# Attention and a routed mixture of experts: a slot table for one expert only, with one scattered row a token tile

## The chip, the cores and the metric

The kernel runs on one core of a Trainium2 chip. The metric is the time of one execution on the device in microseconds (us). Five engines run their own instruction streams: PE (matrix products, with its weight loads shown as PEld), DVE (vector), ACT (scalar functions), POOL (here mostly the issuer of indirect DMAs) and SP (the issuer of plain DMAs). They meet through semaphores.

## The reference

Attention over 8 batches, 8 heads, 576 tokens, head size 64, with a causal window of 32 (first four heads) or a dilated window (reach 128, every fourth key, last four heads). Its output, 4608 tokens of 512 numbers, goes through a mixture of 8 experts, each token through its best two:

```python
logits = x @ w_gate
noise_scale = np.log1p(np.exp(x @ w_noise))
noisy_logits = logits + noise_scale * noise
top2 = np.argpartition(-noisy_logits, 2, axis=1)[:, :2]
top2_l = np.take_along_axis(noisy_logits, top2, axis=1)
top2_l = top2_l - top2_l.max(-1, keepdims=True)
top2_w = np.exp(top2_l)
top2_w /= top2_w.sum(-1, keepdims=True) + 1e-09
for e in range(E):
    for k in range(2):
        mask = top2[:, k] == e
        h = np.maximum(x[mask] @ w1[e], 0.0)
        out[mask] += top2_w[mask, k, None] * (h @ w2[e])
```

## The kernel before

**Attention** runs in 24 steps, four units of 1152 tokens with six steps each (three of each mask type). A step has scores (PE L348), their maximum (DVE L353), exponentials, transposes (PE L368, evicted by ACT L371 as `pt`), the product with the values (PE L388, `o`), the division (DVE L395 to L400), transposes of the result (PE L414, ACT L416) and the gate's logits (PE L436). A step has two places, called slots here and numbered `kb`, between which other work is put: `at(kb, f)` runs `f` in slot `kb`, and generators on the list `gens` are advanced a few instructions at a time by `micro`.

**Gates.** `gate(t0, n)` takes `n` tiles of 128 tokens: it finds the two best experts of each token, counts tokens per expert by a product with a triangular matrix (so every token gets a rank within its expert), and then writes, for each tile and each of the two choices, one row of eight integers per token into the table `tab` in DRAM at row (expert, rank): the four places of the token's attention output in the scratch `xs`, the weight, the token's number. That is an indirect DMA issued by POOL (L577) with a one-element memset ahead of it (L576): two a tile, 72 in all. The gates start at slots 17, 29, 39, 41, 51 with 9, 9, 6, 3, 6 tiles; one of 3 tiles is left for the end of attention. Rows of the table that no token takes are filled beforehand (`setup_c`, L267 to L288; the tokens' places are computed in one block of DVE work, `setup_b`, L226 to L261).

**Experts.** Expert 0 is a fixed one; the other seven are taken in the order of their token counts, and each has a fixed capacity of 1216 down to 1152 slots (an overflow path, which the data here doesn't enter, handles the rest). An expert has three blocks of 3, 4 and 3 tiles. `up` (L764) makes 12 products for each of 8 slices `f` of the hidden size (three for each fourth of the model size, since operands are split in a high and a low part), ACT takes the relu into `hh` (L768) and DVE the low part `hl` (L769). `down_tile` (L805) makes 24 products for a tile, DVE multiplies by the weight into `y` (L814), and POOL adds the rows to the output by an indirect DMA with addition (`out_rows`, L782, with a memset L781). PSUM holds three buffers for `up` and two for `dn`.

**Fetching tokens.** For expert 0 SP reads rows of the table into `ixf`, POOL gathers (four indirect DMAs a tile, L710), and PE transposes (L730). For another expert SP reads its part of the table (`idx_dma`: L688, L691, L693), DVE copies it into place (L698), POOL gathers (L716, one indirect DMA for 32 tokens), and DVE transposes in 32 by 32 squares (L733). ACT and DVE split the result into `x` (L735, L736). Expert 0's first block is fetched during the last unit of attention.

**What sets the order.** Each engine's instructions stand in the order of the code. After attention a clock of column counts (`tick`, 2400 columns a us) decides where planned work (`plan(t, f)`) is put between the products of `up` and `down`.

Of the kernel before, what the change touches and what calls it, by code (L numbers as in the profile page):

```python
# [12 lines left out]
I32 = mybir.dt.int32  # L13
# [27 lines left out]
US_W2 = 3.0, 3.5  # L41
US_X = (17, 52)
# [3 lines left out]
def attention_moe_kernel(ctx, tc, qt, kp, kd, vpl, vdl, w_gate, w_noise, noise, w1, w2, out, CAPS=(1216, 1216, 1216, 1184, 1184, 1152, 1152, 1152), SPLITS=(0, 384, 896)):  # L46
# [19 lines left out]
    xq = xs.rearrange("r (q d) -> (r q) d", d=128)  # L66
    tab = dram.tile([E * ET, TC], I32, name="tab")

# [4 lines left out]
    ixp = ctx.enter_context(tc.tile_pool(name="ixp", bufs=3))  # L73
# [121 lines left out]
    i8 = gat.tile([128, NG, E], F32, name="i8")  # L195
# [5 lines left out]
    def setup_a():  # L201
# [7 lines left out]
        gpsimd.iota(i8, pattern=[[0, NG], [1, E]], base=0, channel_multiplier=0,  # L209
                    allow_small_or_imprecise_dtypes=True)  # L210
        gpsimd.iota(ebase, pattern=[[ET, E]], base=0, channel_multiplier=0,
                    allow_small_or_imprecise_dtypes=True)
        gpsimd.tensor_copy(base, ebase)
        for e in range(E):
# [4 lines left out]
    def setup_b():  # L219
# [3 lines left out]
        t = tokc[:, :, 5]  # L223
        v, s, i0, r, z, a = (acon.tile([128, 2, NT], I32, name=f"tc{i}") for i in range(6))
        gpsimd.iota(v[:, 0].rearrange("p (s j) -> p s j", j=3), pattern=[[0, 12], [128, 3]], base=0, channel_multiplier=1)
        vector.tensor_scalar(a[:, 0], t, 2, None, op0=OP.bitwise_and)  # L226
        vector.tensor_scalar(v[:, 1], t, 2, None, op0=OP.logical_shift_right)
        vector.scalar_tensor_tensor(v[:, 1], a[:, 0], 72.0, v[:, 1], op0=OP.mult, op1=OP.add)
        for u in range(U):
            c = slice(NG * u, NG * u + NG)  # L230
            gpsimd.iota(s[:, 0, c].rearrange("p (s j) -> p s j", j=3), pattern=[[768, 3], [0, 3]],
                        base=768 * (6 * u + 3), channel_multiplier=0)
            vector.tensor_scalar(a[:, 0, c], t[:, c], float(TU * u + S), 144.0, op0=OP.is_ge, op1=OP.mult)
            vector.scalar_tensor_tensor(v[:, 1, c], v[:, 1, c], -288.0 * u, a[:, 0, c], op0=OP.add, op1=OP.add)
            vector.memset(s[:, 1, c], 4608 * u)
# [227 lines left out]


    tabw = []
    LG = {}

    def gate_front(u, st):
        if st == 0:
# [677 lines left out]
```

## Time and profile before

| | |
|---|---|
| median of 3 runs | 1205.72 us (1190.08, 1205.72, 1205.93) |
| the profiled execution | 1184.15 us; its span in the trace 1182.5 us; mean granted clock 0.941 |
| attention, until expert 0's first product | 0 to 265.6 us |
| expert 0 | 265.6 to 418.8 us |
| expert 1 | 418.8 to 540.4 us |
| each later expert | some 106 to 111 us |

Rows of the stretches list, behind the two ends and the length in us, the busy us and the number of instructions of PE, PEld, DVE, ACT and POOL, then the granted clock of PE (1.00 is full), the busy share of the DMA engines and GB/s. Rows of groups list line, engine, operation, tiles, count, then busy us and mean ns, then the engine's idle time ahead of them and what ended most of it. Rows of waits list engine, tile and line, what was waited for, us in total, times, longest.

### The profile page before, as it was taken

To read this page: it belongs to the slowest core of one execution; us is meant where nothing else is said; L and a number is where in the kernel's file an instruction comes from. 1 tells how busy PE (TensorE), PEld (TensorE's weight loads), DVE (VectorE), ACT (ScalarE), POOL (GpSimd) and SP (SyncE) were. 2 spreads that over 40 slices of the span, in tenths; PEclk is the share of its full clock that TensorE was granted. 3 is DMA by queue.
4 is the path that set the end of the run, shared out by engine and by line. 5 is a ranking of instruction groups with operands and counts; after the bars stand their busy time and mean duration, and the time that the engine had idled before them with its cause. 6 is when DMAs were issued, how large, how long until landed. Compare 5 with 4: busy or idle time off the path is not lost. (4 is left out here: it accounts for less than half of the span.)

```text
span 1182.5 us, 18050 instructions
## 1 busy us (share of the span) xinstructions
PE 1026.8 (87%) x7278; PEld 865.2 (73%) x7279; DVE 467.6 (40%) x1077; ACT 298.9 (25%) x540; POOL 519.9 (44%) x637
## 2 busy tenths in 40 slices
PE   5885737667589899899999998999999999999996
PEld 3663535446378787788889887978888898878885
DVE  6762524344223335243432433343434334332321
ACT  6442413342111223122222312231222223122210
POOL 5006062526456453745644562465246445624012
PEclk9997879777699999899999998999999999999998
DMA  8794538437033233352434333343424353432223
GB/s 287 266 331 182 206 126 299 150 127 271 11 62 63 70 94 94 63 115 52 118 56 108 83 89 63 81 107 74 106 47 116 68 97 91 84 94 45 54 28 45
DMA packets 70967, 133.71 MB, mean 113 GB/s; under 512 B 29520, under 2 KB 29568, under 8 KB 69600
## 3 DMA queue, kind: packets, MB, share of 16 engines
q1 hardware_dynamic: 48176, 93.22, 23.4%
q0 software_dynamic: 22704, 39.30, 18.6%
q8 instruction: 58, 0.95, 0.3%
q14 instruction: 29, 0.24, 0.1%
HBM read 92.19 MB, written 40.29 MB: 112 GB/s over the span
## 5 line engine op out<-in xcount | busy, mean ns | idle before, releaser
L764 PE MATMUL up<-x,w1h 128*128 128x512 f32 (+4 forms) x1536 | 403.4, 349 | 43.1 <-issue 16.8
L764 PEld LDWEIGHTS up<-x,w1h 128*128 128x128 f32 x1536 | 278.9, 194 | 70.3 <-DVE hl L769 18.8
L716 POOL DMA_INDIRECT g<-xs,ixi x258 | 259.7, 1007 | 107.9 <-issue 84.2
L764 PE MATMUL up<-x,w1l 128*128 128x384 f32 (+4 forms) x768 | 266.3, 347 | 1.7 <-issue 1.6
L782 POOL DMA_INDIRECT out_rows<-y,ixs x67 | 106.3, 1586 | 310.6 <-DVE y L814 260.9
L805 PE MATMUL dn<-w2h,hh 128*128 128x512 f32 x576 | 227.4, 395 | 3.3 <-issue 1.8
L805 PE MATMUL dn<-w2l,hh 128*128 128x512 f32 x576 | 226.1, 393 | 4.4 <-issue 4.4
L805 PE MATMUL dn<-w2h,hl 128*128 128x512 f32 x576 | 225.9, 392 | 3.0 <-issue 3.0
L769 DVE SCALAR_TENSOR_TENSOR hl<-up,hh 128x384 fp32r<-128x384 f32 (+2 forms) x192 | 105.7, 556 | 299.0 <-ACT hh L768 205.9
L768 ACT ACTIVATE hh<-up 128x384 fp32r<-128x384 f32 (+4 forms) x192 | 92.7, 498 | 320.7 <-PE up L764 197.0
L764 PEld LDWEIGHTS up<-x,w1l 128*128 128x128 f32 x768 | 149.1, 194 | 12.2 <-issue 1.8
L805 PEld LDWEIGHTS dn<-w2h,hl 128*128 128x128 f32 x576 | 109.3, 190 | 27.4 <-issue 4.3
L805 PEld LDWEIGHTS dn<-w2h,hh 128*128 128x128 f32 x576 | 109.5, 190 | 26.9 <-issue 4.3
L805 PEld LDWEIGHTS dn<-w2l,hh 128*128 128x128 f32 x576 | 109.5, 190 | 26.6 <-issue 4.7
L577 POOL DMA_INDIRECT tab<-en,si x72 | 70.2, 975 | 115.1 <-DVE den L397 55.5
L814 DVE TENSOR_SCALAR y<-dn,ixs 128x512 f32<-128x512 f32 x63 | 46.9, 748 | 127.8 <-PE dn L805 121.5
L735 ACT CAST x<-xr 128x512 fp32r<-128x512 f32 x67 | 40.5, 605 | 175.8 <-DVE xr L733 144.1
L649 DVE TENSOR_TENSOR w1l<-ws,w1h 128x1024 fp32r<-128x1024 f32 x32 | 38.7, 1218 | 75.3 <-ACT w1h L647 67.7
L388 PE MATMUL o<-vp,pt 128*32 128x130 f32 x576 | 32.1, 296 | 30.3 <-ACT pt L371 16.7
L710 POOL DMA_INDIRECT g<-xs,ixf x40 | 38.3, 958 | 42.8 <-DMA kt<-in_kp 21.7
L647 ACT CAST w1h<-ws 128x1024 fp32r<-128x1024 f32 x32 | 33.1, 1048 | 92.8 <-DMA ws<-in_moe_w 92.8
L733 DVE STREAM_TRANSPOSE xr<-g 128x512 f32<-128x512 f32 x67 | 45.8, 683 | 20.5 <-DMA g<-xs,ixi 16.2
(184 smaller groups left out, 839.4 us busy)
## 6 DMA issues: line engine op xcount, KB each, us to landing
ws<-in_moe_w SPq DMA_DIRECT2D x64, 512.0 KB
out_rows<-zero SPq DMA_DIRECT2D x38, 256.0 KB
vd<-in_vdl SPq DMA_DIRECT2D x24, 390.0 KB
vp<-in_vpl SPq DMA_DIRECT2D x16, 585.0 KB
xs<-x SPq DMA_DIRECT2D x24, 384.0 KB
qt<-in_qt SPq DMA_DIRECT2D x14, 576.0 KB
kt<-in_kd SPq DMA_DIRECT2D x16, 320.0 KB
g<-xs,ixi POOLq DMA_INDIRECT x258
```

What stands on the lines that cost most here:

```text
L577: ins = gpsimd.indirect_dma_start(out=tab, out_offset=bass.IndirectOffsetOnAxis(ap=si[:, kq, t:t + 1], axis=0), in_=en[:, kq, t], in_offse ...
L649: return lambda: vector.tensor_tensor(b, s, a.bitcast(F32), op=OP.subtract)
L710: gpsimd.indirect_dma_start(out=g[0:rn, c], out_offset=None, in_=xq[0:rows], in_offset=bass.IndirectOffsetOnAxis(ap=IX[0][0][0:rn, t, c:c ...
L716: gpsimd.indirect_dma_start(out=g[:, j], out_offset=None, in_=xq, in_offset=bass.IndirectOffsetOnAxis(ap=IX[e][1][:, r0 // 32 + j:r0 // 32 ...
L733: vector.transpose(xr[:, :, 0:rn].rearrange("p c (g t) -> p g c t", t=32), g[:, 0:n].rearrange("p g (c d) -> p g c d", d=32))
L735: scalar.copy(xh[:, :, o:o + rn], xr[:, :, 0:rn])
L764: tensor.matmul(p[:, 0:n], lhsT=a[:, 128 * f:128 * f + 128], rhs=b[:, kc, 0:n], start=(i == 0), stop=(i == 11))
L768: scalar.activation(hh[:, f, 0:n], p[:, 0:n], AF.Relu)
L769: vector.scalar_tensor_tensor(hl[:, f, 0:m], p[:, 0:m], 0.0, hh[:, f, 0:m].bitcast(F32), op0=OP.max, op1=OP.subtract)
L782: ins = gpsimd.indirect_dma_start(out=out, out_offset=bass.IndirectOffsetOnAxis(ap=sc[0:rn, t, 1:2], axis=0), in_=y[0:rn], in_offset=None, ...
L805: tensor.matmul(p[0:rn], lhsT=a[:, f, o:o + rn], rhs=b[:, f % 2], start=(i == 0), stop=(i == 23))
L814: vector.tensor_scalar(y[0:rn], p[0:rn], wsc, None, op0=OP.mult)
```

## The change

- The table is for expert 0 only (`tab0`). A gate scatters one row a token: to its slot if one of its two choices is expert 0, else to a row beyond the table that nobody reads. That is one indirect DMA a tile (L624), 36 in all.
- There are four gates during attention in place of five (slots 17, 29, 43, 51 with 9, 9, 9, 6 tiles), and the one at the end.
- A gate also keeps each token's (expert, rank) and weight in SBUF and writes the weights of all experts to a DRAM array `wtab` by SP (L592).
- For the other seven experts the slots are found without a table. For each of the 72 pairs of a tile and a choice, two matrices are made: `A`, 128 by 128, one where a token's rank modulo 128 is the column's number, and `V`, 128 by 70, the token's number in the column of its expert and tile of slots, else zero. The product of `A` transposed and `V`, added up over all 72 in one PSUM bank `acc`, is the token of each slot. `A` is made by DVE (odd pairs, L730) or by two ACT instructions (even pairs, L732, L733), `V` by DVE (L734); the product is L739. `slots()` is run through by planned steps during expert 0, and ends with some 59 DVE instructions (L746 to L771) that turn tokens into places in `xs`.
- An expert's gathers (now L878) then take their indices from SBUF: the reads of the table by SP and the 28 copies L698 go. For the weights there is one more gather a tile (`wq` from `wtab`, L884), 67 in all, planned ahead of the `up` of their block.
- Expert 0's first block is gathered in halves of a tile, in twice as many slots; expert 1's gathers are planned from 64.1 instead of 51 on the planner's clock after expert 0's start, and closer together (5 for 7, 15 for 21).
- `token_places` replaces `setup_b`: a generator in small pieces, from slot 8. `setup_c` fills 1280 rows instead of all.

The core of the diff:

```diff
-        for t in range(n):
-            for kq in range(2):
-                gpsimd.memset(spacer, 0.0)
-                ins = gpsimd.indirect_dma_start(
-                    out=tab, out_offset=bass.IndirectOffsetOnAxis(ap=si[:, kq, t:t + 1], axis=0),
-                    in_=en[:, kq, t], in_offset=None)
...
+        for t in range(n):
+            gpsimd.memset(spacer, 0.0)
+            ins = gpsimd.indirect_dma_start(
+                out=tab0, out_offset=bass.IndirectOffsetOnAxis(ap=si[:, t:t + 1], axis=0),
+                in_=en[:, t], in_offset=None)
...
+    def slots():
...
+        acc = late["mps"].tile([128, NO], F32, name="acc", tag="acc", bufs=1)
+        for i in range(m + 3):
+            if i < m:
+                if i % 4 == 0:
+                    av = late["stage"].tile([128, 4, 256], F32R, name="av", tag="ws")
+                A, V = av[:, i % 4, 0:128], av[:, i % 4, 128:128 + NO]
+                if i % 2:
+                    vector.tensor_scalar(A, iof, lo[:, i:i + 1], None, op0=OP.is_equal)
+                else:
+                    scalar.activation(A, iof, AF.Abs, bias=nlo[:, i:i + 1])
+                    scalar.activation(A, A.bitcast(F32), AF.Relu, scale=-1.0, bias=one)
+                vector.tensor_scalar(V, iof[:, 0:NO], d[:, i:i + 1], tokf[:, i // 2:i // 2 + 1],
+                                     op0=OP.is_equal, op1=OP.mult)
+                ops[i] = (A, V)
+            if i >= 3:
+                A, V = ops.pop(i - 3)
+                tensor.matmul(acc, lhsT=A, rhs=V, start=(i == 3), stop=(i == m + 2), skip_group_check=True)
+            yield
...
+    def weights(e, t):
+        c, rn = NC * (e - 1) + t, TLS[e][t][1]
+        gpsimd.indirect_dma_start(out=late["wq"][0:rn, c:c + 1], out_offset=None, in_=wtab,
+                                  in_offset=bass.IndirectOffsetOnAxis(ap=late["wi"][0:rn, c:c + 1], axis=0))
...
-                later(2 + i if bi == 0 else 1, lambda t=t: gather(0, t))
+                for h in range(2):
+                    later(1 + 2 * i + h, lambda t=t, h=h: gather(0, t, (2 * h, 2 * h + 1)))
...
-    for t0, n, kb in ((0, 9, 17), (9, 9, 29), (18, 6, 39), (24, 3, 41), (27, 6, 51)):
+    for t0, n, kb in ((0, 9, 17), (9, 9, 29), (18, 9, 43), (27, 6, 51)):
...
+            bulk = others()
+            for i in range(135):
+                plan(start + BULK[0] + BULK[1] * i, lambda: next(bulk, None))
+            plan(start + BULK[2], lambda: [None for _ in bulk])
...
+                if e:
+                    for i, ti in enumerate(range(BLS[e][bi][0], BLS[e][bi][1])):
+                        plan(now[0] + 1 + 1.5 * i, lambda ti=ti, e=e: weights(e, ti))
                 up((e, bi), X.pop((e, bi)), BLS[e][bi][3], tail(e, bi))
```

Three places of the engines' own orders show what moved. The first is POOL in the last third of attention, where the gates' scatters (memset and `tab`) meet the first gathers of expert 0. Before, eight gathers follow the 36th scatter, four scatters come between, and then four more gathers:

```order
L576 MEMSET spacer 1x1
L577 DMA tab<-en,si 37376x8
L710 DMA g<-xs,ixf 128x128 x8
L576 MEMSET spacer 1x1
L577 DMA tab<-en,si 37376x8
L576 MEMSET spacer 1x1
L577 DMA tab<-en,si 37376x8
L576 MEMSET spacer 1x1
L577 DMA tab<-en,si 37376x8
L576 MEMSET spacer 1x1
L577 DMA tab<-en,si 37376x8
L710 DMA g<-xs,ixf 128x128 x4
```

The same place now: after the 18th scatter stand all twelve gathers, and then the third gate's nine scatters, with nothing between them:

```order
L623 MEMSET spacer 1x1
L624 DMA tab_58<-en,si 9216x8
L871 DMA g<-xs,ixf 128x128 x12
L623 MEMSET spacer 1x1
L624 DMA tab_58<-en,si 9216x8
L623 MEMSET spacer 1x1
L624 DMA tab_58<-en,si 9216x8
```

The twelve gathers have come together, and the scatters ahead of them have gone from 36 to 18.

The second is PE in the second `up` block of expert 0 (128 by 512 results; `w1h` and `w1l` are the high and low parts of the weights, with buffer numbers). Before, one slice's 12 products stand directly behind another's:

```order
L764 MATMUL up<-x,w1h_3100 128x512 x2
L764 MATMUL up<-x,w1l_3101 128x512
L764 MATMUL up<-x,w1h_3142 128x512 x2
L764 MATMUL up<-x,w1l_3143 128x512
L764 MATMUL up<-x,w1h_2842 128x512 x2
L764 MATMUL up<-x,w1l_2843 128x512
```

Now seven products of the 0-1 matrices come between:

```order
L930 MATMUL up<-x,w1h_3006 128x512 x2
L930 MATMUL up<-x,w1l_3007 128x512
L930 MATMUL up<-x,w1h_3039 128x512 x2
L930 MATMUL up<-x,w1l_3040 128x512
L739 MATMUL acc<-av 128x70 x7
L930 MATMUL up<-x,w1h_2698 128x512 x2
L930 MATMUL up<-x,w1l_2699 128x512
```

So it is behind each of the eight slices; the other 16 products stand ahead of the block and among the `dn` products after it.

The third is POOL over one later expert. Before, gathers of the next expert's tokens and scatters of results alternate:

```order
L716 DMA g<-xs,ixi 128x128 x16
L781 MEMSET spacer 1x1
L782 DMA out_rows<-y,ixs 4864x512
L781 MEMSET spacer 1x1
L782 DMA out_rows<-y,ixs 4864x512
L716 DMA g<-xs,ixi 128x128 x4
L781 MEMSET spacer 1x1
L782 DMA out_rows<-y,ixs 4864x512
L716 DMA g<-xs,ixi 128x128 x8
```

Now the weight gathers stand among them:

```order
L878 DMA g<-xs,xi 128x128 x4
L884 DMA wq<-wtab,wi 128x1 x4
L878 DMA g<-xs,xi 128x128 x12
L947 MEMSET spacer 1x1
L948 DMA out_rows<-y,rw 4864x512
L947 MEMSET spacer 1x1
L948 DMA out_rows<-y,rw 4864x512
L878 DMA g<-xs,xi 128x128 x4
```

Four of them make the longest run of gathers 20 long instead of 16.

More of the change, by code (lines that the diff above doesn't have):

```diff
@@ L41 @@
 US_W2 = 3.0, 3.5
+BULK = 15, 0.36, 64
 US_X = (17, 52)
@@ L614, in totals @@
         yield 0
+        vector.tensor_copy(cn, over)
+        yield 0
         vector.tensor_tensor(over, over, capf, op=OP.subtract)
```

430 lines of the change are left out of this document (296 added, 134 removed).

## The prediction

> **What bounds the kernel now.** I began with the first part of the page and the slices.
>
> ```profile
> PE 1026.8 (87%) x7278; PEld 865.2 (73%) x7279; DVE 467.6 (40%) x1077; ACT 298.9 (25%) x540; POOL 519.9 (44%) x637
> PE   5885737667589899899999998999999999999996
> POOL 5006062526456453745644562465246445624012
> ```
>
> PE is the engine nearest its limit, and from the twelfth slice on it is nearly full. In the first third it has holes, and they stand where POOL's digits rise (the fourth and sixth slices, 5 and 3 for PE, 6 and 6 for POOL). The chain that ended last names only the end and tells nothing here, so I went on to stretches. A later expert first, then an attention step with POOL idle, and the same step with POOL busy:
>
> ```profile
> 540.40:649.20 108.80, 105.91 (x522) 91.87 (x521) 43.47 (x75) 25.81 (x43) 55.19 (x59) 1.00 0.40 85
> 129.32:135.94 6.62, 5.95 (x131) 4.93 (x130) 3.67 (x8) 3.14 (x6) 0.00 (x0) 1.00 0.89 314
> 99.50:129.32 29.82, 14.96 (x130) 8.35 (x129) 3.67 (x8) 3.21 (x6) 16.21 (x32) 0.60 0.33 113
> 135.94:143.30 7.36, 5.53 (x128) 4.61 (x127) 4.50 (x12) 3.70 (x11) 0.00 (x0) 1.00 0.75 259
> 151.06:186.58 35.52, 15.77 (x255) 11.90 (x255) 8.55 (x24) 7.14 (x16) 18.75 (x35) 0.71 0.33 116
> ```
>
> Expert 2 leaves PE 2.9 us free in 108.8, so there is little to win there. In attention the same work, some 130 PE and 8 DVE instructions, takes 6.62 us with POOL idle and 29.82 us with POOL issuing; two such steps take 35.52 us where two undisturbed ones take 6.62 + 7.36 = 13.98. What POOL issues in the first of these stretches and in the second, and who waits in the second (150 to 180 us):
>
> ```profile
> L577 POOL DMA_INDIRECT tab<-en,si x18 | 17.4, 969 | 37.4 <-DVE si L572 33.6 <-issue 3.7
> L577 POOL DMA_INDIRECT tab<-en,si x18: 957/962/963, 153.8 to 175.3; - x18
> ACT pt L371 <- remote: 17.8, 1, 17.8
> PE o L388 <- ACT pt L371: 15.9, 2, 15.6
> DVE mx L353 <- remote: 11.2, 1, 11.2
> ```
>
> Both stretches hold one gate's 18 scatters, 153.8 to 175.3 us for the second, one in 1.26 us. Meanwhile ACT waits 17.8 us for something that the trace gives no name ("remote"), PE 15.6 us for ACT, DVE 11.2 us. The DMA engines are a third busy, less than in the undisturbed steps (0.89, 0.75), so bandwidth isn't it. So the bound before 265.6 us is, in places, the length of POOL's run of scatters, and this is what the change halves.
>
> **The change part by part.** First the price of one indirect DMA in a run, from further stretches: eight gathers alone, then twelve scatters with four gathers.
>
> ```profile
> 201.46:215.35 13.89, 9.27 (x135) 6.46 (x134) 5.59 (x32) 3.51 (x10) 4.92 (x7) 0.75 0.86 339
> 215.35:249.92 34.57, 20.90 (x261) 13.14 (x261) 13.81 (x47) 10.77 (x24) 16.72 (x28) 0.75 0.31 99
> ```
>
> The first run loses 29.82 - 6.62 = 23.2 us, 1.29 a scatter; the second 35.52 - 13.98 = 21.5, 1.19; the third 34.57 - 13.98 = 20.6, 1.29 for each of 16; the eight gathers 13.89 - 7.36 = 6.5, 0.8 each. I take 1.24 for a scatter of the first two runs. So, one by one:
>
> 1. Runs one and two go from 18 scatters to 9 each: 18 x 1.24 = -22.3 us. If only the part beyond a fixed start is won, less; if nine cost hardly anything, twice as much (a rival).
> 2. The third run goes from 12 scatters to 9: 3 x 1.29 = -3.9. The twelve gathers now stand directly ahead of it instead of eight and four apart: four more in the first piece, 4 x 0.8 = +3.2, the four in the other piece being priced with the 16 above, so between 0 and +3.2 and I keep +3.2.
> 3. Expert 0's first blocks run under 16 gathers and 12 scatters of POOL (273 to 308 us):
>
> ```profile
> 265.60:297.70 32.10, 22.43 (x105) 20.74 (x103) 12.43 (x65) 5.94 (x12) 21.03 (x27) 0.77 0.73 252
> 523.70:540.50 16.80, 16.80 (x98) 16.78 (x97) 6.70 (x12) 3.60 (x7) 11.84 (x13) 1.00 0.42 111
> 299.30:331.90 32.60, 22.41 (x93) 16.75 (x93) 9.88 (x27) 4.53 (x9) 16.83 (x31) 0.75 0.09 12
> 577.20:593.60 16.40, 16.40 (x74) 13.59 (x73) 5.32 (x8) 2.33 (x4) 8.81 (x10) 1.00 0.39 83
> 321.10:332.20 11.10, 11.10 (x55) 9.16 (x53) 2.90 (x8) 1.17 (x2) 9.47 (x15) 1.00 0.26 32
> ```
>
> The first `up` takes 32.1 us against 16.8 for one of that size elsewhere, the first `dn` 32.6 against 16.4: 31.5 lost over 28 indirect DMAs, 1.1 each. Six of these scatters go: -6.7. The last six (321.1 to 332.2, with two result scatters) cost PE nothing, 11.10 busy of 11.10, so their halving brings 0.
>
> 4. In the second `up`, twelve gathers of the third block now stand ahead of it, among the `dn` products:
>
> ```profile
> 331.70:360.30 28.60, 23.85 (x99) 19.19 (x99) 8.01 (x27) 3.97 (x7) 13.52 (x15) 0.94 0.33 72
> 555.40:577.30 21.90, 21.90 (x98) 18.13 (x97) 12.16 (x16) 8.96 (x13) 17.11 (x18) 1.00 0.48 125
> ```
>
> This `up` loses 28.60 - 21.90 = 6.7 us, most in one gap at the end of that run. Moved, the loss may follow (0) or stay away (-6.7); I take -4, the larger part, since the run of scatters beside them is shorter.
>
> 5. The 72 products, on PE. Here `up` runs as 96 products of 512 columns in 21.9 us and 96 of 384 in 16.8, 53 ns for 128 columns, so 70 columns are worth some 30 ns at the least. The nearest single row is the 128-column transposes, 301 ns of latency each:
>
> ```profile
> L730 PE MATMUL xrp<-ident,g 128*128 128x128 f32 (+1 forms) x40 | 6.9, 301 | 0.8 <-PE dn L805 0.8
> L283 DVE TENSOR_SCALAR free<-free 128x97 int32<-128x97 int32 x8 | 1.2, 248 | 0.0
> L769 DVE SCALAR_TENSOR_TENSOR hl<-up,hh 128x512 fp32r<-128x512 f32 x8 | 5.3, 689 | 20.6 <-ACT hh L768 16.6 <-issue 4.1
> L441 ACT COPY gs<-gp 64x192 f32<-64x192 f32 x24 | 7.6, 315 | 39.0 <-PE gp L436 38.8
> ```
>
> Forty of them kept PE busy 6.9 us, 0.17 each; so 72 lie between 2 and 22 us, and I take 0.1 each, +7, nearer the lower end because seven stand behind one another. Their operands: per slice DVE makes 7 `V` and 3 or 4 `A` at some 0.25 us (the 128x97 row), 2.6 us, and its `hl`, 0.69: 3.3 us. PE's slice takes 21.9 / 8 = 2.74 and 0.7 for seven products: 3.4. ACT's 7 at 0.32 make 2.2, and its relu. DVE and PE come out level, so neither covers the other's delays: I add +5 for eight slices and the pieces around them (0 to 15). In all +12. The 83 further DVE instructions at its head and tail (some 0.2 us) fill a DVE that is idle for more than half of expert 0: 0.
>
> 6. The 67 weight gathers lie on POOL, 9 or 10 an expert at about 1.0 us:
>
> ```profile
> L716 POOL DMA_INDIRECT g<-xs,ixi x258 | 259.7, 1007 | 107.9 <-issue 84.2
> ACT hh L768 <- PE up L764: 7.9, 2, 4.0
> ```
>
> POOL goes from 55 to 65 us of an expert's 109. PE's 2.9 us of idleness fall around the end of a run of 15 indirect DMAs, where ACT's relu waits once 4.0 us for its slice (the row of 600 to 610 us). Runs grow by three or four: 4 x 2.9 / 15 = 0.8, times seven: +5. The ends are 0 (hidden like the six scatters at 321 us) and 28 (a rival). The multiplication `y` now waits for `wq`, with every later `hl` behind it on DVE; the weights are planned a whole `up` ahead, 16.8 us or more, so I price this wait at 0, and in the rival where they come late.
>
> 7. Expert 0's and expert 1's table reads and copies go, expert 1's gathers start later but closer: 0, within 5 either way, covered by `up` and `dn` in between. The setup in pieces instead of a block, and a short fill:
>
> ```profile
> 28.94:37.40 8.46, 6.01 (x127) 4.60 (x127) 7.44 (x48) 3.76 (x10) 0.00 (x0) 1.00 0.60 246
> ```
>
> This step, with 48 DVE instructions, is 1.8 us longer than the 6.62 of the clean one: -2 (0 to -2).
>
> The sum: -22.3 - 3.9 + 3.2 - 6.7 - 4 + 12 + 5 - 2 = -18.7 us, so 1184.15 - 18.7 = 1165.4 us on the profiled execution's scale. That execution stands 21.6 us below the median of the runs shown, whose three spread by 16 us; carried over by the difference, 1205.7 - 18.7 = **1187.0 us**, -1.6%. Two per cent, about what a measurement of this kernel tells from no change, is 24.1 us: faster means below 1181.6, slower above 1229.8.
>
> One rule of the Trainium skill speaks against the largest term. "SBUF — State Buffer", section "Who interferes with whom", has it that only vector and GpSimd engine share ports, and that "PE and ACT never wait on anyone". By that alone POOL's scatters could not hold PE and ACT, and terms 1 to 4 would be worth nothing. The rows of 99.50 to 129.32 us, 23.2 us lost under 18 scatters, say that they are held by something; the rule is about ports, and what the trace calls "remote" need not be one. The skill's rule stays as the ground of the last rival, which I give little.
>
> **The rivals.**
>
> A. *Short runs cost little.* The loss sets in only when a run has gone on for some us. For it: the run of eight at 321 us costs nothing. Against it: eight gathers cost 6.5 us. Then nine scatters are as good as free, and runs one and two give another 22.3: 1187.0 - 22.3 = 1164.7; with the third too (9 x 1.29 = 11.6) 1153.
>
> B. *The weight gathers lengthen the runs that PE already feels.* Four more in a run at 1.0 us, all of it handed on to PE as in expert 0's first blocks (1.1 each), or `y` waiting as long for its weight: 4 us an expert, 28 in place of 5: 1210. It decides where POOL is behind by more than an `up`. For it: the gaps that exist at the ends of runs of 15. Against: an expert's POOL has 40 us free.
>
> C. *The products tie PE to late signals: slower than before.* Each group waits in PE's order for DVE and ACT. If a signal under POOL's runs comes 4.0 us late, as that relu's did, each of ten groups (eight slices, and those ahead and behind) stops PE: 40 in place of 5, 1187.0 + 35 = 1222. It decides if POOL still issues a run (the twelve gathers, or expert 1's sixteen) while the products run. Against: the three pairs of lag between making and using.
>
> D. *Fewer scatters don't free PE.* What holds the steps is then not the number of scatters, which only lie beside it (the change doesn't do what it seems to). Terms 1 to 4 vanish and 5 to 7 remain: 1205.7 + 15 = 1221. Against it: four stretches with a loss in proportion to the count.
>
> **How the numbers follow.** The forecast gets 0.45, A 0.24, B 0.13, C 0.12, D 0.06. The range takes in the forecast's own ends (1173 to 1203, from the bounds of terms 1, 4, 5 and 6), A but for its farthest part, and B; of C and D half: **1152 to 1222**. Faster by over 2%: nearly all of A and a third of the forecast, 0.38; slower: the far part of C and D, 0.08; within 2%: 0.54.
>
> **What would show it.** Two runs of nine scatters in attention, each with a loss near 11 us for the step around it (A: under 4; D: still above 20). The first `up` and `dn` of expert 0 some 7 us shorter together. The second `up` with seven `acc` products behind each slice at 25 to 30 us (C: over 50), PE waiting there for `av`. Later experts at 107 to 111 us (B: 112 to 115), DVE's `y` not waiting for `wq`. The forecast is wrong above all if the loss isn't linear in the run's length, or if the products' partners come late.

## The result, and the profile after

The changed kernel took 1294.65 us (median of 4 runs, 1292.64 to 1298.11), the kernel before beside it 1200.9 (1190.08 to 1205.93): a ratio of 1.080, 95% interval 1.071 to 1.089. The forecast was 1187, the range ended at 1222. One thing must be known to read the runs below: in some sets of runs the kernel before took 1182 to 1206 us, as here (the condition of the prediction), in others 1053 to 1062 (the other condition), and one chip showed both, so every run is read against the kernel before of its own set, and its traces against the trace of its kind.

The page of the changed kernel's profiled execution (1298.11 us, span 1296.3): busy time and instructions by engine, then PE and POOL in the 40 slices.

```profile
PE 1076.3 (83%) x7349; PEld 898.5 (69%) x7350; DVE 501.9 (39%) x1219; ACT 322.5 (25%) x609; POOL 540.2 (42%) x628
PE   6787577857887768789899979997899798889995
POOL 5002230455054725356615653464546347424221
```

The holes of the first third have become shallower, but PE now has holes over the whole second half, where it was nearly full. The time from one expert's first `up` product to the next one's (worked out from the traces) says where the 113.8 us of the two spans came from:

| us | attention | expert 0 | 1 | 2 | 3 | 4 | 5 | 6 | 7 | tail |
|---|---|---|---|---|---|---|---|---|---|---|
| before | 265.6 | 153.2 | 104.9 | 108.8 | 110.9 | 106.3 | 105.9 | 106.9 | 111.0 | 9.0 |
| changed | 244.9 | 178.7 | 129.7 | 124.1 | 122.0 | 122.4 | 124.9 | 124.2 | 112.3 | 13.2 |
| difference | -20.7 | +25.5 | +24.8 | +15.3 | +11.1 | +16.1 | +19.0 | +17.3 | +1.3 | +4.2 |

The table goes by `up` products: expert 2's first one stands at 523.7 us in the kernel before, and the 540.4 us given ahead of the prediction as expert 1's end is the first `dn` product behind it. The differences are between two single executions, and that of the kernel before is the fastest known in this set (1184.15 us for a median of 1200.9): by medians the change cost 93.8 us, and which stages hold the other 20 isn't known.

Attention, in stretches of the changed kernel's trace: a step with nine scatters (seven of them inside), the clean one after it, a step with the second nine, one under the twelve gathers (the first falls ahead of it); then expert 2, its last `up` alone, and the end of that `up`.

```profile
105.21:122.14 16.93, 11.43 (x131) 7.04 (x130) 3.67 (x8) 3.11 (x6) 6.69 (x14) 0.70 0.56 206
122.14:128.74 6.60, 5.93 (x130) 4.92 (x130) 3.67 (x8) 3.13 (x6) 0.00 (x0) 1.00 0.97 346
143.87:160.71 16.84, 5.73 (x127) 4.60 (x127) 4.54 (x20) 3.57 (x10) 9.30 (x17) 0.80 0.66 221
182.42:202.79 20.37, 11.46 (x127) 7.22 (x127) 3.40 (x7) 3.24 (x9) 9.80 (x12) 0.66 0.71 278
553.20:677.30 124.10, 111.46 (x521) 95.01 (x520) 45.18 (x76) 26.24 (x44) 64.35 (x68) 0.94 0.33 75
630.80:655.50 24.70, 17.15 (x98) 16.18 (x97) 6.99 (x19) 3.99 (x9) 14.33 (x17) 0.80 0.25 48
649.00:655.50 6.50, 3.59 (x14) 3.55 (x14) 2.79 (x8) 1.72 (x4) 0.00 (x0) 0.50 0.30 43
```

Nine scatters cost 16.93 - 6.60 = 10.3 us where eighteen cost 23.2: nearly in proportion, as forecast. Inside a run it isn't even: PE kept its rate through the first five scatters (24 products from 106 to 108 us, 3 from 110 to 112), and the granted clock stayed at 0.50 until 119 us, 6 us after the run. Expert 2 does the same 521 products as before (522) in 124.1 us instead of 108.8. Of these 15.3 us PE is idle for 9.7 (12.6 for 2.9); the other 5.6 are products that took longer (111.46 us busy for 105.91) at a granted clock of 0.94 for 1.00. The last row shows where: behind the stretch in which PE had little to do, the clock was 0.50. The changed kernel's rows of waits, first in that last `up` (630.8 to 655.5 us), then inside a long run of POOL in expert 1 (441 to 464 us):

```profile
ACT hh L934 <- remote: 9.9, 2, 7.4
```

```profile
ACT hh L934 <- remote: 20.1, 2, 16.4
PEld up L930 <- issue: 15.8, 4, 13.6
```

The relu is ready to run when its slice is done, and starts 7.4 and 16.4 us late, for no reason that the trace names. Set against POOL's instructions, these delays have a pattern. In a run of indirect DMAs that follow one another without a pause, the relu of a product that ends early in the run starts as usual (0.04 us after its last product). In the traces of the two kernels the first late relu has four DMAs of its run ahead of it (1.4 us late), and most have eight to thirteen. From there on a relu can be late by up to 22.4 us (kernel before, product end at 281.1 us), and at the latest it runs some 4 us after POOL's run has ended. Before, an expert's runs had some 11, 15 and 18 DMAs; with the weight gathers they have some 14, 18 and 22, and in expert 1 one has 27 (429.2 to 464.1 us). So the weight gathers lengthen each run at its late end. That was theory 1: what counts is the length of an unbroken run. The expectations below name three others: theory 2, that it is something else than the weight gathers; theory 3, that gathering single numbers is costly in itself; theory 4, that it is the pace at which indirect DMAs are issued.

### The profile page after: what moved, and what is told of

Same layout as the page of the kernel before. It is cut to its first block, busy times and chain, and to the rows that moved or that the text cites. A ratio compares the mean times of both kernels' runs of the same rounds, so it can differ in the third digit from the quotient of the medians.

```text
span 1296.3 us, 18374 instructions
## 1 busy us (share of the span) xinstructions
PE 1076.3 (83%) x7349; PEld 898.5 (69%) x7350; DVE 501.9 (39%) x1219; ACT 322.5 (25%) x609; POOL 540.2 (42%) x628
## 5 line engine op out<-in xcount | busy, mean ns | idle before, releaser
L930 PE MATMUL up<-x,w1h 128*128 128x512 f32 (+4 forms) x1536 | 421.3, 360 | 95.8 <-issue 35.8
L930 PEld LDWEIGHTS up<-x,w1h 128*128 128x128 f32 x1536 | 289.0, 202 | 128.7 <-issue 60.4
L878 POOL DMA_INDIRECT g<-xs,xi x258 | 251.9, 976 | 82.1 <-issue 76.5
L930 PE MATMUL up<-x,w1l 128*128 128x384 f32 (+4 forms) x768 | 273.6, 356 | 5.9 <-issue 5.2
L948 POOL DMA_INDIRECT out_rows<-y,rw x67 | 106.4, 1588 | 359.7 <-DVE y L980 328.1
L971 PE MATMUL dn<-w2h,hh 128*128 128x512 f32 x576 | 231.5, 402 | 6.7 <-issue 6.6
L930 PEld LDWEIGHTS up<-x,w1l 128*128 128x128 f32 x768 | 155.1, 202 | 19.8 <-issue 8.1
L971 PEld LDWEIGHTS dn<-w2h,hh 128*128 128x128 f32 x576 | 111.9, 194 | 34.1 <-issue 11.7
L624 POOL DMA_INDIRECT tab<-en,si x36 | 35.4, 983 | 161.6 <-DVE rx L619 115.2
L980 DVE TENSOR_SCALAR y<-dn,wq 128x512 f32<-128x512 f32 x63 | 47.0, 748 | 121.5 <-PE dn L971 106.8
L884 POOL DMA_INDIRECT wq<-wtab,wi x67 | 68.0, 1015 | 20.4 <-issue 17.7
L899 DVE STREAM_TRANSPOSE xr<-g 128x512 f32<-128x512 f32 x67 | 45.8, 683 | 30.0 <-DMA g<-xs,xi 25.2
```

The lines of the kernel that those rows point to most:

```text
L878: gpsimd.indirect_dma_start(out=g[:, j], out_offset=None, in_=xq, in_offset=bass.IndirectOffsetOnAxis(ap=ix, axis=0))
L884: gpsimd.indirect_dma_start(out=late["wq"][0:rn, c:c + 1], out_offset=None, in_=wtab, in_offset=bass.IndirectOffsetOnAxis(ap=late["wi"][0: ...
L899: vector.transpose(xr[:, :, 0:rn].rearrange("p c (g t) -> p g c t", t=32), g[:, 0:n].rearrange("p g (c d) -> p g c d", d=32))
L930: tensor.matmul(p[:, 0:n], lhsT=a[:, 128 * f:128 * f + 128], rhs=b[:, kc, 0:n], start=(i == 0), stop=(i == 11))
L948: ins = gpsimd.indirect_dma_start(out=out, out_offset=bass.IndirectOffsetOnAxis(ap=row_, axis=0), in_=y[0:rn], in_offset=None, compute_op= ...
L971: tensor.matmul(p[0:rn], lhsT=a[:, f, o:o + rn], rhs=b[:, f % 2], start=(i == 0), stop=(i == 23))
```

## The experiments

**1. Four parts at once.** The first leaves the weight gathers out and sets the weights to 0.5:

```diff
-                if e:
-                    for i, ti in enumerate(range(BLS[e][bi][0], BLS[e][bi][1])):
-                        plan(now[0] + 1 + 1.5 * i, lambda ti=ti, e=e: weights(e, ti))
...
+    vector.memset(late["wq"], 0.5)
```

> The changed kernel without its 67 weight gathers; the weights of experts 1 to 7 are set to 0.5 once, so the output isn't the reference's. Theory 1 (the gathers make POOL's unbroken runs of indirect DMAs longer, and signals between engines come late from some 9 us into a run): experts 2 to 7 fall from 730 us together to some 635, expert 1 by some 8, the whole from 1295 to about 1190 to 1200. Theory 2 (experts 2 to 7 are slower for another reason, such as later gathers of tokens or the lower clock that the products leave): 1270 or more.

The second moves them for experts 2 to 7:

```diff
             if pend:
                 pend.pop(0)()
+            if 0 < e < E - 1 and t < len(TLS[e + 1]):
+                weights(e + 1, t)
             down_tile(e, (e, bi), r0 - s0, rn, t, rn <= 64)
```

> All weight gathers are there, but those of experts 2 to 7 are issued one at a time, behind the result scatter of each down tile of the expert before, where POOL has pauses. Theory 1 (length of the run): most of the loss goes, experts 2 to 7 at 640 to 665 us together for 730, the whole 1215 to 1240. Theory 3 (a weight gather of 128 single numbers is costly in itself, wherever it stands): no gain beyond 15 us, 1280 or more.

The third paces the scatters of the kernel before:

```diff
-                gpsimd.memset(spacer, 0.0)
+                for _ in range(12):
+                    gpsimd.memset(spacer, 0.0)
                 ins = gpsimd.indirect_dma_start(
                     out=tab, out_offset=bass.IndirectOffsetOnAxis(ap=si[:, kq, t:t + 1], axis=0),
```

> The kernel before, with twelve one-element memsets instead of one ahead of each of the gates' 72 scatters, so that a scatter is issued every 2.0 to 2.5 us instead of every 1.27. Theory 4 (rate: each indirect DMA leaves something that drains more slowly than it comes, so what counts is the pace): the runs of 18 lose 0 to 5 us instead of 21 to 23, expert 0's first product at 205 to 235 us instead of 265.6, the whole 1130 to 1175. Theory 1 in its strict form (what counts is how long POOL issues without a real pause): the runs are 40 us long instead of 22, and lose more, first product at 290 or later, the whole above 1215.

The fourth drops the loop over the 72 products in `slots()`:

```diff
-        for i in range(m + 3):
...
-        vector.tensor_scalar(tk, acc, float(HALF), None, op0=OP.add)
+        vector.tensor_copy(by(tk), rank.unsqueeze(1).to_broadcast([128, E - 1, NC]))
```

> The changed kernel without the 72 products of 0-1 matrices and what makes their operands; the slots hold tokens 0, 1, 2 and so on, so the output isn't the reference's. If the products cost what expert 0 has gained in time beside the runs: the second up falls from 42.1 to 22 to 29 us, expert 0 from 178.6 to 155 to 165 us, the whole by 15 to 25 to some 1273. If POOL's runs make the loss there too: the second up stays above 35 us, the whole falls by under 8.

Measured: 1070.0, 1071.7, 1147.9 and 1048.7 us, beside 1057.4 for the kernel before. All expectations were written for 1200, and nothing of theory 1 could be seen: with or without weight gathers experts 2 to 6 took 99 to 105 us. Two things follow. The products, with what makes their operands, are dear by themselves: without them expert 0 takes 115.6 us, with them 135.3 to 136.8 in every run of this kind, some 20 to 21 us. And a pause of twelve memsets is too much: with one scatter in 2.8 us attention ends at 244.6 us, and expert 0 waits for its tokens (172.8 us, PE once 31.2 us for a gather).

**2. Both kernels as they are, and the products spread.** The fourth kernel of this set stages the planned work after each fourth of a slice:

```diff
                     i += 1
-            tick(12 * n)
+                if key == (0, 1):
+                    tick(3 * n)
+            if key != (0, 1):
+                tick(12 * n)
```

> The changed kernel as it is, beside the kernel before on one chip. Where the kernel before takes about 1200 us: 1280 to 1310 again. Where it takes about 1057 us, as beside the last four kernels, signals between engines are hardly late under POOL's runs, so by theory 1 the weight gathers cost little: 1070 to 1085, the loss being that of the products in expert 0 alone. By theory 3 (a weight gather is costly in itself): 1140 or more there too.

> The kernel before as it is, for its trace. If the difference between some 1200 and 1057 us is how late signals come under POOL's runs, and not the clock or the memory: with 1057 us, attention ends near 200 to 215 instead of 265.6, expert 0 takes 115 to 125 instead of 153, experts 2 to 7 some 607 instead of 633, and relu starts within 1 us of its product's end in nearly all slices. If it is the clock alone: all stages shorter by the same share, 12%.

> The changed kernel with the weight gathers of experts 2 to 7 one at a time behind the result scatters. Theory 1: where the kernel before takes about 1200, 60 to 85 us less than the changed kernel; where it takes about 1057, within 8 us of it. Theory 3: within 15 us of the changed kernel in both.

> As the last one, and in the second up block of expert 0 the products of 0-1 matrices stand one or two at a time between the fourths of a slice instead of seven behind it. If PE waits there because the operands of a group of seven are made too late (DVE and ACT need some 3.3 us for seven, and only eight are held at a time): that up falls by 4 to 9 us (from 31.4 to 23 to 27 where the kernel before takes about 1057). If DVE and ACT are simply too slow for 72 operands in that time: within 2 us, the wait only moves.

Measured: 1077.0, 1056.6, 1069.8, 1064.3, beside 1062.1. The trace of the kernel before, now in the other condition: the stretches of a run of 18 scatters and of expert 2, and then POOL's group of scatters in the first.

```profile
98.20:120.80 22.60, 19.41 (x403) 16.06 (x399) 13.50 (x29) 10.48 (x24) 18.88 (x36) 1.00 0.92 333
421.20:526.40 105.20, 105.20 (x521) 91.88 (x520) 46.05 (x80) 26.36 (x44) 56.20 (x58) 1.00 0.42 90
```

```profile
L577 POOL DMA_INDIRECT tab<-en,si x18 | 17.4, 967 | 37.7 <-DVE si L572 34.0 <-issue 3.7
```

The same 18 scatters, 967 ns each, one in 1.26 us, and PE gets through 403 products where it got through 75 in the trace that the prediction read. No relu is late by more than 0.1 us in the whole trace, though runs have up to 36 DMAs. So a run of POOL holds the other engines only in a condition which this kernel doesn't set; attention then ends at 197.8 us, expert 0 takes 127.9, experts 2 to 6 take 99 to 105 (the first two lie outside the ranges expected, 200 to 215 and 115 to 125). Attention is a quarter shorter, experts 2 to 6 are 2% to 7% shorter: not a common factor, hence not the clock alone (0.941 and 0.982 on average). In this condition the change has nothing to win with its scatters: attention 201.4 for 197.8, expert 0 136.8 for 127.9, the tail 13.3 for 9.2.

In the second `up` of expert 0 spreading the products gave 29.0 for 31.5 us. That `up` in the changed kernel as it is, as a stretch, and its group of products (241 to 278 us):

```profile
241.20:272.70 31.50, 29.71 (x150) 24.58 (x149) 23.17 (x86) 20.83 (x55) 17.67 (x22) 1.00 0.29 47
```

```profile
L739 PE MATMUL acc<-av 128*128 128x70 f32 x61 | 10.1, 271 | 3.9 <-ACT av L733 2.3 <-DVE av L734 1.3
```

The gain is less than the 4 to 9 expected: PE waits only 3.9 us for operands, and the 61 products keep it busy for 10.1 us, 0.17 each; without them this `up` takes 23.9 (21.9 in the kernel before).

**3. Timed in turn.**

> The changed kernel timed in turn with the kernel before on one chip. Where the kernel before takes about 1057 us (signals in time under POOL's runs): ratio 1.010 to 1.022, the loss in expert 0's products and at the end. Where it takes about 1200 (signals late): 1.06 to 1.09.

> The changed kernel with the weight gathers of experts 2 to 7 one at a time behind result scatters and the products spread in the second up block. Where the kernel before takes about 1057: ratio 1.000 to 1.010. Where it takes about 1200: by theory 1 (the length of POOL's runs) 0.97 to 1.02; by theory 3 (a weight gather is costly in itself) 1.05 or more.

Measured, beside 1056.4 us: 1068.5, ratio 1.011 (1.009 to 1.013), and 1065.1, ratio 1.008 (1.006 to 1.010). Both as expected for 1057.

**4. In the condition of the prediction: weights moved, products spread wider.** The edit is the planner's step, 0.45 for 0.36, and fourths of a slice in the third `up` too.

> As the spread products before, with the planned steps 0.45 instead of 0.36 of the planner's us apart, so that they reach into the third up, where they also stand in fourths of a slice. Where the kernel before takes about 1057: if PE still waits for operands, another 2 to 5 us gained, 1059 to 1063; if not, 1063 to 1066. Where it takes about 1200: by theory 1 (length of POOL's runs) 1160 to 1220, by theory 3 (a weight gather is costly in itself) 1260 or more.

Measured: 1272.7 beside 1198.9, ratio 1.062. That is neither theory 1's 1160 to 1220 nor the changed kernel's 1295, and on its face theory 3's (1260 or more). The trace says why it doesn't decide: experts 2 to 6 took 122.2, 117.0, 116.1, 114.0, 123.2 us, and the run that costs most, at each expert's third `up`, was as long as before the move, 18 DMAs in 24.3 us (622.3 to 646.6; in the changed kernel 624.6 to 648.9), since POOL was behind there and the moved gathers only changed places in it. Nor was all else alike: against the changed kernel's trace experts 2 to 6 are 25.2 us shorter together and expert 0 is 9.8 shorter, but expert 1 is 12.5 longer (142.2 us, its longest run 32 DMAs instead of 27). Where a run did get shorter, the products beside it did too: the `up` of 384 columns of experts 4 and 5 went from 20.2 and 23.3 to 16.8 and 17.2 us.

**5. Another treatment for each expert.** One kernel, so all is compared under one condition:

```diff
+        if e == 2:
+            return
+        if e == 4:
+            gpsimd.indirect_dma_start(out=spare[t % 4], out_offset=None, in_=xq,
+                                      in_offset=bass.IndirectOffsetOnAxis(ap=late["xi"][:, c, 0:1], axis=0))
+            return
+        if e == 5:
+            return
...
+            if STG[0] == 5:
+                for _ in range(8):
+                    gpsimd.memset(spacer, 0.0)
```

> The changed kernel with another treatment of POOL in each of five experts, timed from an expert's first up product to the next one's. Expert 2: no weight gathers. Expert 3: as in the changed kernel. Expert 4: in place of each weight gather of single numbers a gather of 128 rows of 512 bytes into tiles no longer needed. Expert 5: no weight gathers, and eight one-element memsets ahead of each gather of tokens (one in about 2 us instead of 1.25). Expert 6: each weight gather twice. The weights of experts 2, 4 and 5 are 0.5, so the output isn't the reference's. Before and changed, where the kernel before takes about 1200: 108.8, 110.9, 106.3, 105.9, 106.9 and 124.1, 122.0, 122.4, 124.9, 124.2 us. There theory 1 (unbroken runs get too long, whatever they gather) expects 107 to 112, 120 to 124, 118 to 124, then 115 or more for expert 5 since its runs get longer, and 133 to 148 for expert 6. Theory 4 (the pace of the indirect DMAs) the same but for expert 5: 105 to 107. Theory 3 (the gather of single numbers) the same as theory 1 but for expert 4: 106 to 110. Where the kernel before takes about 1057: all five within 2 us of 104, no theory told apart.

Measured: 1089.8, where the kernel before takes 1056.4; experts 2 to 6 took 105.4, 104.1, 104.6, 116.8, 105.6. Eight memsets starve an expert of tokens, and nothing is told apart. The same with four:

> The changed kernel with another treatment of POOL in each of five experts, timed from an expert's first up product to the next one's: expert 2 no weight gathers, expert 3 as in the changed kernel, expert 4 gathers of 128 rows of 512 bytes in place of the weight gathers, expert 5 no weight gathers and four one-element memsets ahead of each gather of tokens, expert 6 each weight gather twice. The weights of experts 2, 4 and 5 are 0.5, so the output isn't the reference's. Where the kernel before takes about 1200: theory 1 (length of the unbroken runs) 107 to 112, 120 to 124, 118 to 124, 112 or more, 133 to 148; theory 4 (pace) the same but 104 to 108 for expert 5; theory 3 (single numbers) the same as theory 1 but 106 to 110 for expert 4. Where it takes about 1057: 105, 104, 104, 104 to 110, 99 to 106.

Measured: 1259.2 beside 1201.1. The five experts as stretches of its trace:

```profile
549.40:659.10 109.70, 106.51 (x522) 91.99 (x521) 44.63 (x74) 26.34 (x44) 56.10 (x59) 1.00 0.39 85
659.10:779.10 120.00, 111.38 (x522) 94.86 (x521) 42.70 (x71) 25.16 (x43) 64.21 (x69) 0.94 0.36 80
779.10:901.60 122.50, 111.53 (x522) 94.78 (x521) 42.51 (x71) 25.39 (x43) 63.99 (x72) 0.93 0.36 81
901.60:1005.40 103.80, 102.91 (x522) 88.42 (x521) 41.34 (x61) 24.89 (x42) 62.02 (x196) 1.00 0.38 82
1005.40:1134.60 129.20, 109.92 (x506) 92.30 (x505) 40.31 (x60) 24.91 (x41) 69.01 (x73) 0.91 0.32 71
```

Without weight gathers expert 2 is back at 109.7 (108.8 before, 124.1 changed), the products left as they are: the gathers are the loss, and theory 2 falls. Expert 4 with gathers of 512-byte rows in their place loses as much as with single numbers, 122.5 for 122.4: theory 3 falls. Expert 6 with each gather twice takes 129.2, 22 more than before for 18 more DMAs, but only 5.0 more than with nine (124.2), and less than the 133 to 148 that every theory gave it: the loss doesn't grow by the same step with each DMA. And expert 5 takes 103.8 us, PE 102.9 us busy. Most of the difference to the changed kernel's 124.9 comes from its weight gathers being left out; what the pause adds shows against the kernel before, which has none either: 2.1 us less (105.9), of the 3.2 that lie above the 102.7 of the other condition. No relu in it starts more than 0.2 us late, though its runs are up to 30 us long. By theory 1 it was to take 112 us or more, so theory 1 falls too in its strict form. That leaves theory 4, the pace: with one indirect DMA in 1.62 us the relus are in time, with one in 1.25 us, in long runs, they aren't.

**6. The same pause everywhere.** Four memsets ahead of every scatter of the gates and every gather of tokens, in the kernel before and in the changed one (which has the spread products and moved weights):

```diff
+            for _ in range(4):
+                gpsimd.memset(spacer, 0.0)
             gpsimd.indirect_dma_start(out=g[:, j], out_offset=None, in_=xq,
```

> The kernel before with four one-element memsets ahead of every scatter of the gates and every gather of tokens (one in about 1.6 us instead of 1.25). Where the kernel before takes about 1200: theory 4 (pace) 1065 to 1110, attention ending at 200 to 220 us, experts 2 to 6 at 100 to 106 each; theory 1 (length of unbroken runs) 1200 or more. Where it takes about 1057: no gain, 1057 to 1085, since POOL has more to do in expert 0.

> The changed kernel with the products spread, the weight gathers of experts 2 to 7 behind the result scatters, and the same pause ahead of scatters and gathers of tokens. Where the kernel before takes about 1200: theory 4 1065 to 1110, within 20 us of the paced kernel before, since half the scatters are worth little once they don't hold anything; theory 1 1250 or more. Where it takes about 1057: 1062 to 1085.

Measured, beside 1188.4 us: the kernel before, paced, 1130.3, ratio 0.953 (0.948 to 0.958); the changed one, paced, 1133.1, ratio 0.956 (0.951 to 0.962). Both are faster than both kernels of the case under this condition, short of the 1065 to 1110 expected. Of the 57 us between the traces of the kernel before and its paced form, 47 lie in attention. The stages are 218.3, 154.3, 107.5, then 99.0 to 107.5 for experts 2 to 6, against 212.8, 137.2, 117.1, then 100.1 to 110.5. A run of 18 scatters in the paced kernel before:

```profile
99.50:129.00 29.50, 21.11 (x379) 16.59 (x380) 10.22 (x23) 8.79 (x20) 21.51 (x85) 0.88 0.68 234
218.30:372.60 154.30, 123.17 (x562) 102.77 (x561) 50.74 (x157) 25.95 (x48) 113.99 (x393) 0.88 0.37 98
```

In 29.5 us PE now does 379 products where it did 130 in 29.8, and 17 of the 18 scatters lie in it. What the relus waited for without a name, over the whole traces of the kernel before and of the changed one (us in total, times, longest):

```profile
ACT hh L768 <- remote: 76.1, 20, 11.6
ACT hh L934 <- remote: 161.4, 26, 16.4
```

Neither paced kernel has such a row, and none of their 192 relus starts more than 0.2 us late. This is the plainest sign for theory 4, though under this condition still: the only waits of that kind left in the paced kernel before are three in attention, 5.1 us at most (17.8 before). What is short of the expectation is expert 0 of the kernel before (154.3, nothing won): its POOL has 72 scatters and 40 gathers to issue by then, and at 1.6 us each the tokens are late. There the change has its use, since it has half the scatters: attention and expert 0 are 22.7 us shorter together. It gives that back in expert 1 (117.1 for 107.5), in experts 2 to 6 (11.7 us together) and in the tail (4.3), with its weight gathers on POOL beside the pauses.

**7. How large a pause.** The first of this set gives 1, 2, 3, 4 and 0 memsets to experts 2 to 6 of the changed kernel, weight gathers included, through a `DOSE` by expert; the second halves the pause of the paced changed kernel.

> The changed kernel with 1, 2, 3, 4 and 0 one-element memsets ahead of each gather of tokens and of weights in experts 2, 3, 4, 5 and 6 (a gather every 1.27, 1.35, 1.48, 1.62 and 1.25 us). Where the kernel before takes about 1200, theory 4 (pace): 120 to 125 us, 114 to 122, 106 to 114, 104 to 109, 122 to 126; a threshold would show as one step from some 122 to some 106. Theory 1 (length of unbroken runs): none below 120. Where it takes about 1057: 105, 104, 104, 104 to 108, 99 to 101.

> The paced changed kernel with two memsets instead of four ahead of scatters and gathers of tokens. Where the kernel before takes about 1188 to 1200: if 1.35 us is slow enough, 1100 to 1125, since POOL has time left in expert 1; if signals are still late at that pace, 1150 to 1230. Where it takes about 1057: 1060 to 1072.

Measured, beside 1054.1: 1093.7, and 1074.6 (above the 1060 to 1072 expected), ratio 1.019 (1.016 to 1.023). The five experts took 105.2, 105.5, 110.3, 112.3, 99.0, for 105.2, 103.8, 103.8, 102.7, 99.0 in the kernel before: with nearly 50 gathers an expert, POOL has time for two memsets (a gather every 1.33 us), not for three (1.48). The same kernel again:

> The changed kernel with 1, 2, 3, 4 and 0 one-element memsets ahead of each gather of tokens and of weights in experts 2, 3, 4, 5 and 6 (measured: a gather every 1.25, 1.33, 1.48, 1.62 and 1.25 us). Where the kernel before takes about 1200, theory 4 (pace): 120 to 126 us, 112 to 122, 108 to 114, 110 to 115 (POOL is full there), 122 to 126. Theory 1 (length of unbroken runs): none below 120. Where it takes about 1057, as the last time: 105.2, 105.5, 110.3, 112.3, 99.0.

Measured: 1084.5 beside 1053.0, again the condition in which no pause helps; the five experts came within 1 us of the last time. From which pace on signals are late is open.

## Why the prediction was wrong

**Terms 1 and 2, the scatters: right.** The loss went nearly with the count, 10.3 and 10.2 us for the steps around the two runs of nine (forecast near 11), and attention ended 20.7 us earlier, against -25 by the terms that fall in it (-22.3 - 3.9 + 3.2 - 2). Most of the difference is the twelve gathers: 20.37 us for a step of 7.36, 13.0 lost, 6.5 more than the eight lost, where I added 3.2. That the loss is in proportion at nine and at eighteen hides that the first five or so of a run cost little and the later ones more; two counts alone can't tell the two apart. Rivals A and D fall: nine scatters weren't free, and fewer did free PE.

**Term 6, the weight gathers: the step that failed.** I priced them at 0.8 us an expert, 5 in all, and rival B at 28. In experts 2 to 6 alone the difference is 78.8 us, and without them expert 2 had its old time back (109.7 for 108.8). The mechanism was in the forecast, as rival B; the size was wrong, in two ways. I divided the gap that a run of 15 makes (2.9 us) by its 15 DMAs. But the early ones of a run cost little, and those that lengthened it cost 1.1 to 2.1 us each (11.1 us for ten in expert 3, 19.0 for nine in expert 5), about a third of it as products at a lower clock (5.6 of 15.3 us in expert 2). And both prices took one run an expert, four gathers; all nine or ten lengthen three runs. A hint was in the prediction: eight DMAs free at 321 us, and 1.19 to 1.29 us each in runs of 16 to 18 (though eight gathers in attention cost 0.8 each). An average over a run isn't what one more costs; nor is one more always the same, since the second nine of experiment 5 added only 5.0 us. The wait of `y` for its weight, priced at 0, was 0: no row of waits of the changed kernel has it.

**Terms 3 to 5, expert 0: wrong by 24 us.** Forecast +1.3, measured +25.5. Its first `up` and `dn` got shorter together, 38.1 + 21.9 for 32.1 + 32.6, 4.7 us of the 7 forecast. The second `up` took 42.1 us (forecast 25 to 30, rival C over 50): in the other condition 31.5 (21.9 without products in the kernel before), so some 10 us are the products; the rest, some 11 us, I put down to late signals, as rival C had it, by the waits in the trace; no run without the products was made under this condition. The stretch, and who waits in it longest for nothing that the trace names:

```profile
304.50:350.70 46.20, 36.62 (x162) 29.38 (x160) 25.56 (x98) 24.74 (x66) 8.50 (x11) 0.89 0.12 19
```

```profile
ACT av L732 <- remote: 12.6, 1, 12.6
DVE av L734 <- remote: 6.7, 1, 6.7
```

Both waits end at 316.7 us, 1.7 us after the run of POOL that holds the twelve gathers of the third block (296.4 to 315.0 us): the loss that term 4 took to stay away for the larger part moved along with the gathers.

By the run without products all that belongs to them costs 20 to 21 us in expert 0 even where signals are in time, against the 12 of term 5. The products are 0.17 us each on PE there (13.3 us for all 72 in the changed kernel's own trace; I took 0.1, though the row of the transposes said 0.17), and the `dn` and `up` after are 2.7 and 6 us longer than without them.

**Term 7: wrong at two places.** Expert 1's gathers, closer together and next to the weight gathers, made the longest run of all (27 DMAs, 13.6 us of PE's weight loads idle in one piece), and expert 1 lost 24.8 us where I wrote 0 within 5. In the other condition it lost 1.0 (96.5 for 95.5); which of its DMAs cost it here wasn't tried. And the tail grew by 2.8 to 4.3 us in every run of the changed kernel. In the traces of the case POOL's closing semaphore instruction starts 5.8 us after the last product instead of 2.3, after six semaphore instructions instead of four; what it waits for there, the trace doesn't name.

**The rule on ports** (the Trainium skill, "SBUF — State Buffer", "Who interferes with whom": PE and ACT wait on no one) disagrees with the relu's 16.4 us and with every run in which POOL issues at full pace under this condition; it agrees with those in the other one, where no relu of the kernel before is late by more than 0.1 us. As a statement on ports it isn't touched, since which resource is held was not found.

**What stays open**: what sets the condition; which resource makes signals late; the pace at which it begins; whether a pause made of something else than memsets does the same; and why the paced kernel before, with its relus in time, still takes 1130 us where the other condition gives 1057 (expert 0, short of tokens, is 26 us of it, attention 21). Shown are that the same kernel has both conditions, that added indirect DMAs without pauses make the loss of experts 2 to 6, that it is the same for the two contents tried, and that pauses bring the relus back in time.

## What to carry to other kernels

A transfer that is off the critical path still has a price if what issues it is already in a series: look for the point in the series from which the other engines are late, and price one more there, not at the mean. Where the profile shows waits with no name while one engine issues DMAs back to back, try a pause between them before moving work to save some: here pauses gave 4.7% under the condition of the prediction, and the rearrangement, paced alike, nothing beyond it. In the other condition they gave nothing: half the pause took the changed kernel from a ratio of 1.008 to 1.019. And time both kernels in more than one set of runs, since a loss that a profile shows may belong to the condition in which it was taken.

## What the runs showed of the hardware that I had not expected

- While indirect DMAs were issued one in 1.25 us, signals of other engines came late from the fifth to the thirteenth on (the relu by up to 22.4 us in the kernel before), and PE got through few products (19 from 104 to 120 us in the kernel before); with one in 1.62 us no relu was late by more than 0.2 us (1130.3 us for 1188.4 in the kernel before).
- The loss has a second part in the clock: in expert 2 of the changed kernel it was 0.50 in the 6.5 us behind a stretch in which PE had little to do, and 5.6 of 15.3 us are products that took longer.
- This comes and goes: the kernel before took 1182 to 1206 us in one condition and 1053 to 1062 in the other, with the same 967 ns a scatter.
- Scatters of 32-byte rows, gathers of 512-byte rows and of single numbers occupy POOL alike, 0.96 to 1.02 us for 128 of them; gathers of the latter two weigh alike in the loss (122.5 and 122.4 us in expert 4).
